# Forgetting attention and a GELU MLP: decay weights by a reversed product scan, v's first pieces among the first loads

## The chip, the cores and the metric

The kernel runs on one core of a Trainium2 chip. The metric is the device time of one execution in microseconds (us). Four executions of the kernel before took 341.31, 341.33, 342.79 and 345.06 us; their median is 342.06. The span is the time between the first and the last instruction in a profiled execution.

The core has five engines that run side by side and meet only at semaphores: TensorE (PE, matrix products; its weight loads are listed apart as PEld), VectorE (DVE), ScalarE (ACT, activation functions), GpSimd (POOL) and SyncE (SP, which here only issues transfers). Each engine takes its own instructions strictly in the order in which the program wrote them. Transfers (DMA) are issued by SP or by POOL and are then carried out by 16 DMA engines that all queues share.

## The reference

Attention over 8 batches, 8 heads, 576 positions and 64 dimensions, in which each key is weakened by the product of all forget factors f after it, followed by a two-layer MLP with an exact GELU over all 4608 tokens.

```python
scores = scale * np.matmul(q, k.transpose(0, 1, 3, 2))
log_f = np.log(np.clip(f, 0.0001, 1.0))
cum = np.cumsum(log_f, axis=-1)
decay = cum[:, :, :, None] - cum[:, :, None, :]
scores = np.where(causal, -1000000000.0, scores + decay)
attn = softmax(scores)                     # max-subtracted, written out in full
x = (attn @ v), heads side by side         # 4608 x 512
h = x @ w_in                               # 512 x 2048
out = gelu(h) @ w_out                      # 2048 x 512
```

For one query the term `cum[query]` is the same for every key and cancels in the softmax. What remains is a weight for each key, proportional to `exp(-cum[key])`. Any common factor of these weights cancels too, because the attention output is divided by the sum of the weights.

## The kernel before

**Tiling.** A head has 576 positions, taken as five key blocks of 128 that start at 0, 128, 256, 384 and 448 (`K0`); the last block is used only in its upper half. Heads are handled in pairs, so that a batch has four pairs, `i` = 0 to 3. `scores(b, i, t)` computes one of four score tiles of a pair on PE (keys on partitions, line 299) and applies Exp on ACT (line 309), giving the tiles `e`. There are two PSUM buffers for score tiles, so PE can be at most two tiles ahead of ACT. `attend` multiplies e by the weighted values `vw` (line 330, called AV below), with the weight itself as a 65th column, which gives the sum. `normalize` (lines 343 and 344, DVE) divides by it and gives x. `to_xT` transposes x on PE (line 363) and copies it out (line 366) on DVE or ACT. `gemm1` (line 385) and `gelu` (line 405) follow, then the second GEMM (lines 421, 479 and 517).

**The weights of the keys.** f is loaded for all 64 batch-heads as one tile of 64 x 576. DVE clamps it (line 185), ACT takes Ln (line 186), DVE scans it to a cumulative sum `cum` (line 188), and ACT computes `wk = Exp(cum[288] - cum)` (line 566). Five PE transposes (line 576) put `wk` on the partitions of the keys, and DVE copies it to `wT` (lines 580, 581). `weigh_v(b, i, eng)` (line 268) multiplies v of a pair of heads by `wT` and gives `vw`. For batch 0 pairs 0 and 1 are weighed on DVE, and pairs 2 and 3 on POOL.

**Order of the loads of batch 0.** q and k are loaded by POOL in pairs of heads, in bf16 (line 107). v is loaded by SP in pieces, one for each key block and half of the heads (`load_v`, line 119). SP has no other work at first, so v is held back by hand: a memset of one column of `v_sb` on POOL (line 151) must run before the first piece may overwrite it, and the pieces after it wait in SP's queue. POOL's queue therefore sets when v starts. In the same way POOL's `gate` (line 546), a copy of one column of v, holds the loads of `w_in` back until v's last piece for heads 0 to 3 has landed.

**Order of the first attention.** `first_attention` is one order written by hand. Warm-up matmuls run on PE until q arrives; then come the transposes of q and k of pair 0 (`transposes_first`, line 207, with copies at 216 to 221), scores of pair 0, transposes of pair 1, and so on. Each engine's order follows the order of the calls. Near the end the calls are `to_xT` of pairs 0 and 1, AV of head (3,0), `to_xT` of pair 2, AV of head (3,1), and the start of GEMM 1, which transposes x of pair 3 in between (`gemm1_begin`). Batches 1 to 7 interleave scores and AV with the second GEMM of the batch before; their code is unchanged.

Of the kernel before, what the change touches and what calls it, by code (L numbers as in the profile page):

```python
# [20 lines left out]
K0 = [0, 128, 256, 384, 448]  # L21
# [31 lines left out]
def kernel(  # L53
# [41 lines left out]
    def load_qk_tokens(b, h0=0, h1=H, which="qk"):  # L95

        if b >= B:
            return
        if b not in qk_of:
            qk_of[b] = [  # L100
                qk_pool.tile([PT, H, JT * D], BF16, tag=n, name=f"{n}{b}")
                for n in "qk"
            ]
        for n, src, dst in zip("qk", (q, k), qk_of[b]):
            if n not in which:
                continue
            nc.gpsimd.dma_start(  # L107
                dst[:, h0:h1, :],
                src[b, h0:h1].rearrange("h (p j) d -> p h (j d)", j=JT),
            )  # L110

    v_sb = consts.tile([P, H, NBLK, D], FP32)

    def load_v(b, h0=0, h1=H):
        if b >= B:
            return
        for n in range(NBLK):
            p0 = D if n == NBLK - 1 else 0
# [29 lines left out]
    diagonal(key_of, Alu.not_equal, 1.0, D)  # L148
    ident_bf = key_of[:, D : D + P]
    load_qk_tokens(0, 4, 6)  # L150
    nc.gpsimd.memset(v_sb[:, :, 0, 0:1], 0.0)
    load_v(0, 0, 4)
    diagonal(after, Alu.is_ge, -1.0e9, D)
    e4 = [consts.tile([P, 2, 448], BF16, name=f"e4{i}") for i in range(4)]
    for t in e4:
        nc.gpsimd.memset(t[:, :, 0:D], 0.0)
    diagonal(ident_fp, Alu.not_equal, 1.0, 0)
    load_qk_tokens(0, 6, 8)
    load_v(0, 4, 8)

    qT = [consts.tile([P, S], BF16, name=f"qT{i}") for i in range(HP)]
    kT = [consts.tile([P, S], BF16, name=f"kT{i}") for i in range(HP)]
# [13 lines left out]


    wT = consts.tile([P, NBLK, BH], FP32)
    ones = consts.tile([BH, S], FP32)
    lf = f_sb  # L180
    cum = consts.tile([BH, S], FP32)
    wk = f_sb
    nc.vector.memset(ones, 1.0)
    nc.vector.memset(wT[0:D, 4, :], 0.0)
    nc.vector.tensor_scalar(f_sb, f_sb, 1e-4, 1.0, Alu.max, Alu.min)
    nc.scalar.activation(lf, f_sb, Act.Ln)
    nc.vector.memset(v_sb[0:D, :, 4, :], 0.0)
    nc.vector.tensor_tensor_scan(cum, ones, lf, 0.0, Alu.mult, Alu.add)
    spark = consts.tile([1, 1], FP32)
    nc.scalar.activation(spark, ones[0:1, 0:1], Act.Exp)  # L190

    def warm_up(n):

        ps = m_psum.tile([P, TC], FP32, tag="m", name="ps_w")
        for _ in range(n):
            nc.tensor.matmul(ps, warm[:, 0:P], warm, start=True, stop=True)

    tails = consts.tile([P, n_dm, TC], BF16)

# [1 line left out]
    def transposes_first(b, i, which, pool, tag):  # L201

        src = qk_of[b][which]
        ps = pool.tile([P, JT, PT], BF16, tag=tag, name="ps_f")
        for j in range(JT):
            for h in range(2):
                nc.tensor.transpose(  # L207
                    ps[h * D : (h + 1) * D, j, :],
                    src[:, 2 * i + h, j * D : (j + 1) * D],
                    ident_bf[:PT, :PT],  # L210
                )

        dst = (qT, kT)[which][i].rearrange("d (p j) -> d p j", j=JT)
        src = ps.rearrange("d j p -> d p j")
        if b or i:
            nc.vector.tensor_copy(dst, src)
        elif which:
            nc.vector.tensor_copy(dst[:, 0 : PT // 2], src[:, 0 : PT // 2])
            nc.scalar.copy(dst[:, PT // 2 :], src[:, PT // 2 :])
        else:  # L220
            nc.scalar.copy(dst, src)
# [41 lines left out]
    def weigh_v(b, i, eng=nc.gpsimd):  # L263

        hs = slice(2 * i, 2 * i + 2)
        bh = b * H + 2 * i
        w = wT[:, :, bh : bh + 2].rearrange("p n h -> p h n")
        eng.tensor_tensor(  # L268
            vw(b)[:, hs, :, 0:D],
            v_sb[:, hs, :, :],  # L270
            w.unsqueeze(3).to_broadcast([P, 2, NBLK, D]),
            Alu.mult,
        )
        if b:
            eng.tensor_copy(vw(b)[:, hs, :, D], w)
# [277 lines left out]
    def first_attention():  # L553


        def transposes(i, pool, tag):
            transposes_first(0, i, 0, pool, tag)
            transposes_first(0, i, 1, pool, tag)

        def attend_head(i, h):  # L560
            attend(0, i, h, (0, 1, 2, 3, 4))
            normalize(0, i, h)

        warm_up(9)
        transposes(0, o_psum, "o")
        nc.scalar.activation(
            wk, cum, Act.Exp, bias=cum[:, S // 2 : S // 2 + 1], scale=-1.0
        )
        warm_up(2)
        scores(0, 0, 0)  # L570
        scores(0, 0, 1)
        transposes(1, m_psum, "m")
        scores(0, 0, 2)
        psw = o_psum.tile([P, NBLK, BH], FP32, tag="o", name="psw")
        for n in range(NBLK):
            nc.tensor.transpose(
                psw[:, n, :], wk[:, K0[n] : K0[n] + P], ident_fp[:BH, :BH]
            )
        scores(0, 0, 3)
        nc.vector.tensor_copy(wT[:, 0:4, :], psw[:, 0:4, :])  # L580
        nc.vector.tensor_copy(wT[D:P, 4, :], psw[D:P, 4, :])
        nc.vector.tensor_copy(
            vw(0)[:, :, :, D], wT[:, :, 0:H].rearrange("p n h -> p h n")
        )
        scores(0, 1, 0)
        transposes(2, m_psum, "m")
        scores(0, 1, 1)
        scores(0, 1, 2)
        scores(0, 1, 3)
        transposes_first(0, 3, 0, m_psum, "m")  # L590
        scores(0, 2, 0)
        transposes_first(0, 3, 1, m_psum, "m")
        weigh_v(0, 0, nc.vector)
        weigh_v(0, 1, nc.vector)
        gate(0, 4)
        load_w_in(0)
        load_w_in(1)
        weigh_v(0, 2)
        weigh_v(0, 3)
        load_w_in(2)  # L600
        nc.gpsimd.memset(v_sb[:, :, 0, 0:1], 0.0)
        load_v(1, 0, 4)
        load_w_in(3)
        load_qk_tokens(1, 0, 4)
        load_qk_tokens(1, 4, 8)
        load_w_out(0)
        scores(0, 2, 1)
        heads = [(i, h) for i in range(3) for h in range(2)]
        for i, t in ((2, 2), (2, 3), (3, 0), (3, 1), (3, 2), (3, 3)):
            scores(0, i, t)  # L610
            attend_head(*heads.pop(0))
        to_xT(0, 0, nc.vector.tensor_copy)
        to_xT(0, 1, nc.scalar.copy)
        attend_head(3, 0)
        both = s_psum.tile([P, 2, 1024], BF16, tag="s", name="ps_x2")
        to_xT(0, 2, nc.scalar.copy, ps=both[:, 0, 0:XC])
        attend_head(3, 1)
        gemm1_begin(0, both)

# [196 lines left out]
```

## Time and profile before

| | us |
|---|---|
| median of four executions | 342.06 |
| the profiled execution | 341.31 |
| its span | 339.5 |
| first attention, to the first full run of GEMM 1 | 0 to 24.9 |
| PE busy in the whole span | 325.1 |
| ACT busy in the whole span | 209.9 |

Stages are read by the time from the start of the span. The profile of the kernel gives the busy time of each engine, the span in 40 slices, and a chain of waits: beginning with the last instruction, it goes back at each step to what released it. The timeline lists instructions in order of time: start, duration, engine, line, operation, tile written and tile read, their shapes, how many were merged into the row, and in brackets the idle time of the engine before it and what ended that time. A duration of a merged row covers all its instructions. The lines on transfer queues give packets, megabytes, and the time that the packets took as a share of 16 engines' time; q0 is POOL's queue and q1 is SP's.

Transfers of the first loads, from issue to landing, by the answers on transfers: q and k of pair 0 were issued at 1.40 and 2.21 and landed after 3.6 and 3.5 us; pair 1 at 2.83 and 3.45, after 4.3 and 4.4; pair 2 at 4.71 and 5.37, after 4.2 and 4.6; pair 3 at 7.22 and 7.87, after 5.2 and 6.5. f was issued at 0.81 and landed after 2.9. The five pieces of v for heads 0 to 3 were issued by SP one after another until 9.8, and took 4.3 to 6.6 us each.

### The profile page before, as it was taken

The page shows a single profiled execution, that of the slowest core. Times are in us where ns is not written, and L with a number is a line of the kernel's source. Part 1 is how long each engine was busy: PE and PEld are TensorE (multiplying, and loading weights), DVE is VectorE, ACT ScalarE, POOL GpSimd, SP SyncE. Part 2 cuts the span into 40 slices and gives each one's busy share as a digit, 9 for nine tenths or more (in the row PEclk, how much of TensorE's full clock was granted, in tenths as well). Part 3 has the DMA queues.
Part 4 walks back from the last instruction along what each step waited for, and adds up shares of the span by engine and source line. Part 5 has one row for each costly group of instructions (what it writes and reads, how often), then busy time and mean ns, then how long its engine had stood idle before and what let it go on. Part 6 is the DMA issues. An engine that isn't in the chain of part 4 may idle for free.

```text
span 339.5 us, 7794 instructions
## 1 busy us (share of the span) xinstructions
PE 325.1 (96%) x3129; PEld 171.6 (51%) x3170; DVE 184.2 (54%) x417; ACT 209.9 (62%) x299; POOL 121.8 (36%) x250
## 2 busy tenths in 40 slices
PE   8699899999999999999999999999999999999995
PEld 4574455445554456445654565446544654444443
DVE  5770456664358935895579646974696541020011
ACT  6977786773734787368737873787368755404600
POOL 8180386037337043723453344524351420000000
PEclk9999999999999999999999999999999999999999
DMA  7999999979999799398959598769900231011013
GB/s 113 184 175 193 209 184 116 217 139 175 216 176 181 112 196 192 96 139 126 229 130 139 106 212 165 97 118 220 159 32 2 82 78 45 0 63 64 0 38 88
DMA packets 104628, 44.18 MB, mean 130 GB/s; under 512 B 83408, under 2 KB 100048, under 8 KB 104592
## 3 DMA queue, kind: packets, MB, share of 16 engines
q1 hardware_dynamic: 87296, 29.52, 46.0%
q0 software_dynamic: 16896, 13.63, 26.8%
q8 instruction: 25, 0.41, 0.5%
q10 hardware_dynamic: 400, 0.52, 0.4%
q14 instruction: 11, 0.09, 0.1%
HBM read 36.85 MB, written 9.44 MB: 136 GB/s over the span
## 4 chain that ended last, share of the span: by engine, by line
PE 89%; issue 3%; ACT 2%; SPq 1%; POOL 1%; DVE 1%; DMA 1%; POOLq 0%; ACTq 0%
PE ps L385 36%; PE ps L479 26%; PE o L330 10%; PE ps L421 8%; PE s L299 7%; ACT e L309 2%; PE ps L517 2%; SPq L119 1%; DMA v_sb<-in_v_dram 1%; PE ps_x L363 1%; POOL q L107 1%; POOL k L107 0%; PE ps_f L207 0%; DVE x L344 0%; DVE vw L268 0%
## 5 line engine op out<-in xcount | busy, mean ns | idle before, releaser
L405 ACT ACTIVATE g<-ps 128x512 bf16<-128x512 f32 x144 | 82.1, 601 | 80.3 <-PE ps L385 80.3
L309 ACT ACTIVATE e<-s 128x896 bf16<-128x896 f32 (+2 forms) x128 | 100.9, 834 | 27.0 <-PE s L299 25.0
L385 PE MATMUL ps<-xT,w_in_sb 128*128 128x512 bf16 x502 | 111.8, 379 | 0.5
L479 PE MATMUL ps<-w_out_sb,g 64*128 64x512 bf16 (+1 forms) x712 | 101.9, 376 | 0.8 <-issue 0.5
L385 PEld LDWEIGHTS <-w_in_sb 128*128 128x128 bf16 x576 | 56.0, 98 | 67.5 <-issue 1.8
L311 POOL TENSOR_SCALAR_AFFINE_SELECT e<-e 128x256 bf16<-128x256 bf16 (+1 forms) x135 | 49.1, 383 | 95.0 <-ACT e L309 94.6
L479 PEld LDWEIGHTS <-g 64*128 64x128 bf16 (+1 forms) x736 | 41.9, 94 | 39.8 <-issue 9.0
L299 PE MATMUL s<-qT,kT 64*128 64x320 bf16 (+4 forms) x384 | 45.4, 276 | 3.3 <-ACT e L309 2.0
L268 POOL TENSOR_TENSOR vw<-v_sb,wT 128x640 bf16<-128x640 f32 x30 | 38.6, 1286 | 23.7 <-DMA v_sb<-in_v_dram 15.2
L249 DVE COPY qT<-tq 64x288 bf16<-64x288 bf16 x96 | 41.4, 431 | 2.9 <-DMA tq<-q 1.5
L249 DVE COPY kT<-tk 64x288 bf16<-64x288 bf16 x96 | 41.5, 432 | 2.5 <-DMA tk<-k 0.9
L487 DVE COPY ot<-ps 128x512 f32<-128x512 f32 x25 | 17.3, 692 | 41.9 <-PE ps L479 41.9
L330 PE MATMUL o<-vw,e 128*128 128x65 bf16 x960 | 36.6, 194 | 3.4 <-issue 2.4
L330 PEld LDWEIGHTS <-e 128*128 128x128 bf16 x960 | 34.1, 98 | 7.3 <-POOL e L311 2.5
L344 DVE TENSOR_TENSOR x<-o,r 128x320 bf16<-128x320 f32 x64 | 31.4, 491 | 2.2
L430 DVE COPY ot<-ps 128x512 f32<-128x512 f32 (+2 forms) x9 | 5.7, 632 | 48.9 <-PE ps L421 46.1
L299 PEld LDWEIGHTS <-kT 64*128 64x128 bf16 x384 | 19.7, 94 | 23.8 <-issue 11.2
L421 PE MATMUL ps<-w_out_sb,g 128*128 128x512 bf16 (+2 forms) x142 | 27.9, 355 | 0.1
L343 DVE RECIPROCAL r<-o 128x5 f32<-128x5 f32 x64 | 12.1, 189 | 22.9 <-PE o L330 22.7
L421 PEld LDWEIGHTS <-g 128*128 128x128 bf16 x144 | 13.5, 98 | 14.5
L490 DVE TENSOR_TENSOR ot<-ot,ps 128x512 f32<-128x512 f32 x25 | 17.2, 687 | 1.4
L385 PE MATMUL ps<-tails,w_in_sb 128*128 128x512 bf16 x62 | 14.2, 377 | 0.2
(67 smaller groups left out, 133.3 us busy)
## 6 DMA issues: line engine op xcount, KB each, us to landing
out_dram<-ot SPq DMA_DIRECT2D x32, 256.0 KB, 2.6
v_sb<-in_v_dram SPq DMA_DIRECT2D x24, 256.0 KB, 4.9
q<-in_q_dram POOLq DMA_DIRECT2D x6, 576.0 KB, 6.4
k<-in_k_dram POOLq DMA_DIRECT2D x6, 576.0 KB, 8.4
v_sb<-in_v_dram SPq DMA_DIRECT2D x22, 128.0 KB, 4.9
w_in_sb<-in_moe_w_in_dram POOLq DMA_DIRECT2D x4, 512.0 KB, 8.4
w_out_sb<-in_moe_w_out_dram POOLq DMA_DIRECT2D x4, 512.0 KB, 8.7
q<-in_q_dram POOLq DMA_DIRECT2D x4, 144.0 KB, 4.2
```

The source lines that it names most:

```text
L249: nc.vector.tensor_copy(rows[:, odd], src[odd * D : (odd + 1) * D, 2 * i + h].rearrange("d j p -> d p j"),)
L268: eng.tensor_tensor(vw(b)[:, hs, :, 0:D], v_sb[:, hs, :, :], w.unsqueeze(3).to_broadcast([P, 2, NBLK, D]), Alu.mult,)
L299: nc.tensor.matmul(to, *ab, start=half < 0, stop=half == 1 or not masked)
L309: nc.scalar.activation(et[:, :, z:c], st[:, :, z:c], Act.Exp, scale=scale)
L311: nc.gpsimd.affine_select(out=et[:, :, c0 + z : c0 + P], in_=et[:, :, c0 + z : c0 + P], compare_op=Alu.is_ge, fill=0.0, base=z, pattern=[[ ...
L330: nc.tensor.matmul(o[:, m, :], e_of[b, i, t][:, h, c : c + P], vw_of[b][:, 2 * i + h, n, :], start=(n == 0), stop=(n == m),)
L344: nc.vector.tensor_tensor(x_of[b, i][:, :, h, :], o[:, :, 0:D], r.unsqueeze(2).to_broadcast([P, NBLK, D]), Alu.mult,)
L385: nc.tensor.matmul(ps, w_in_sb[:, kt, ffb * P : (ffb + 1) * P], src[:, kt, 0:TC], start=(kt == 0), stop=(kt == n_dm - 1),)
L405: nc.scalar.activation(g_of[c][ffb], ps, Act.Gelu)
L421: nc.tensor.matmul(pss[ts][:, c0:c1], g_of[c][kt][:, ts * P : (ts + 1) * P], w_out_sb[:, kt, c0:c1], start=(kt == 0), stop=(kt == n_ff - 1),)
L479: nc.tensor.matmul(banks[r], g_of[c][kt][rows, ts * P : (ts + 1) * P], w_out_sb[rows, kt, :], start=kt == (steps.index("r") if r else 0), ...
L487: nc.vector.tensor_copy(ot, banks[1])
```

## The change

The decay weights become a product. Since common factors cancel, the weight of a key may be the product of all later f, which one scan gives when it runs backwards: `decay[575] = 2**80`, `decay[s-1] = decay[s] * f[s]`. The scan reads f and writes `decay` through reversed views; its added operand is a tile of zeros, `none`. Ln, `cum` and the Exp at line 566 go, and the spark, a one-element Exp that loads ACT's table, comes first. The factor 2**80 keeps products of up to 575 factors in the range of the type.

The memsets of `e4`, and those that hold v back, move from POOL to DVE. `load_v` gets a parameter that selects key blocks. Blocks 0 and 1 of heads 0 to 3 are issued after a DVE memset near the start; blocks 2 to 4 and the second half of the heads after another, which stands behind the scan. On POOL, q and k of pair 3 are issued right after the mask `after`, ahead of `ident_fp`. In the first attention the second warm-up has 256 columns, `weigh_v(0, 0)` stands ahead of the transposes and the copy of k of pair 3, and `to_xT` of pair 2 stands ahead of AV of head (3,0).

```diff
-    def load_v(b, h0=0, h1=H):
+    def load_v(b, h0=0, h1=H, ns=range(NBLK)):
...
-        for n in range(NBLK):
+        for n in ns:
...
     load_qk_tokens(0, 4, 6)
-    nc.gpsimd.memset(v_sb[:, :, 0, 0:1], 0.0)
-    load_v(0, 0, 4)
     diagonal(after, Alu.is_ge, -1.0e9, D)
-    e4 = [consts.tile([P, 2, 448], BF16, name=f"e4{i}") for i in range(4)]
-    for t in e4:
-        nc.gpsimd.memset(t[:, :, 0:D], 0.0)
+    load_qk_tokens(0, 6, 8)
     diagonal(ident_fp, Alu.not_equal, 1.0, 0)
-    load_qk_tokens(0, 6, 8)
-    load_v(0, 4, 8)
...
-    ones = consts.tile([BH, S], FP32)
-    lf = f_sb
-    cum = consts.tile([BH, S], FP32)
-    wk = f_sb
-    nc.vector.memset(ones, 1.0)
+    none = consts.tile([BH, S], FP32)
+    decay = consts.tile([BH, S], FP32)
+    nc.vector.memset(none, 0.0)
+    spark = consts.tile([1, 1], FP32)
+    nc.scalar.activation(spark, none[0:1, 0:1], Act.Exp)
+    nc.vector.memset(v_sb[:, 0:4, 0, 0:1], 0.0)
+    load_v(0, 0, 4, (0, 1))
+    nc.vector.memset(v_sb[0:D, :, 4, :], 0.0)
     nc.vector.memset(wT[0:D, 4, :], 0.0)
+    nc.vector.memset(decay[:, S - 1 : S], 2.0**80)
+    e4 = [consts.tile([P, 2, 448], BF16, name=f"e4{i}") for i in range(4)]
+    for t in e4:
+        nc.vector.memset(t[:, :, 0:D], 0.0)
     nc.vector.tensor_scalar(f_sb, f_sb, 1e-4, 1.0, Alu.max, Alu.min)
-    nc.scalar.activation(lf, f_sb, Act.Ln)
-    nc.vector.memset(v_sb[0:D, :, 4, :], 0.0)
-    nc.vector.tensor_tensor_scan(cum, ones, lf, 0.0, Alu.mult, Alu.add)
-    spark = consts.tile([1, 1], FP32)
-    nc.scalar.activation(spark, ones[0:1, 0:1], Act.Exp)
-
-    def warm_up(n):
+    nc.vector.tensor_tensor_scan(
+        decay[:, S - 2 :: -1],
+        f_sb[:, S - 1 : 0 : -1],
+        none[:, 0 : S - 1],
+        2.0**80,
+        Alu.mult,
+        Alu.add,
+    )
+    nc.vector.memset(v_sb[:, 0:4, 2, 0:1], 0.0)
+    load_v(0, 0, 4, (2, 3, 4))
+    load_v(0, 4, 8)
+
+    def warm_up(n, w=TC):
...
         transposes(0, o_psum, "o")
-        nc.scalar.activation(
-            wk, cum, Act.Exp, bias=cum[:, S // 2 : S // 2 + 1], scale=-1.0
-        )
-        warm_up(2)
+        warm_up(2, 2 * P)
...
-                psw[:, n, :], wk[:, K0[n] : K0[n] + P], ident_fp[:BH, :BH]
+                psw[:, n, :], decay[:, K0[n] : K0[n] + P], ident_fp[:BH, :BH]
...
         scores(0, 2, 0)
+        weigh_v(0, 0, nc.vector)
         transposes_first(0, 3, 1, m_psum, "m")
-        weigh_v(0, 0, nc.vector)
         weigh_v(0, 1, nc.vector)
...
         to_xT(0, 1, nc.scalar.copy)
-        attend_head(3, 0)
         both = s_psum.tile([P, 2, 1024], BF16, tag="s", name="ps_x2")
         to_xT(0, 2, nc.scalar.copy, ps=both[:, 0, 0:XC])
+        attend_head(3, 0)
         attend_head(3, 1)
```

More of the change, by code (lines that the diff above doesn't have):

```diff
@@ L178 @@
     wT = consts.tile([P, NBLK, BH], FP32)
-    ones = consts.tile([BH, S], FP32)
-    lf = f_sb
-    cum = consts.tile([BH, S], FP32)
-    wk = f_sb
-    nc.vector.memset(ones, 1.0)
+    none = consts.tile([BH, S], FP32)
[6 more added lines that the diff above has]
+    nc.vector.memset(v_sb[0:D, :, 4, :], 0.0)
     nc.vector.memset(wT[0:D, 4, :], 0.0)
+    nc.vector.memset(decay[:, S - 1 : S], 2.0**80)
+    e4 = [consts.tile([P, 2, 448], BF16, name=f"e4{i}") for i in range(4)]
+    for t in e4:
+        nc.vector.memset(t[:, :, 0:D], 0.0)
     nc.vector.tensor_scalar(f_sb, f_sb, 1e-4, 1.0, Alu.max, Alu.min)
-    nc.scalar.activation(lf, f_sb, Act.Ln)
-    nc.vector.memset(v_sb[0:D, :, 4, :], 0.0)
-    nc.vector.tensor_tensor_scan(cum, ones, lf, 0.0, Alu.mult, Alu.add)
-    spark = consts.tile([1, 1], FP32)
-    nc.scalar.activation(spark, ones[0:1, 0:1], Act.Exp)
-    def warm_up(n):
+    nc.vector.tensor_tensor_scan(
[10 more added lines that the diff above has]
+    def warm_up(n, w=TC):
         ps = m_psum.tile([P, TC], FP32, tag="m", name="ps_w")
         for _ in range(n):
-            nc.tensor.matmul(ps, warm[:, 0:P], warm, start=True, stop=True)
+            nc.tensor.matmul(
+                ps[:, 0:w], warm[:, 0:P], warm[:, 0:w], start=True, stop=True
+            )
     tails = consts.tile([P, n_dm, TC], BF16)
```

## The prediction

> **What bounds the kernel now.** I begin with the page's busy table, its slices and its chain.
>
> ```profile
> span 339.5 us, 7794 instructions
> ...
> PE 325.1 (96%) x3129; PEld 171.6 (51%) x3170; DVE 184.2 (54%) x417; ACT 209.9 (62%) x299; POOL 121.8 (36%) x250
> ...
> PE   8699899999999999999999999999999999999995
> ...
> PE 89%; issue 3%; ACT 2%; SPq 1%; POOL 1%; DVE 1%; DMA 1%; POOLq 0%; ACTq 0%
> ```
>
> TensorE (PE) is busy for 96% and carries 89% of the chain. No edit takes real work from PE except 0.3 us of warm-up, so the change can win only where PE waits. Every edit acts before 24.4 us. I therefore read busy time by stage (first attention to 24.4 us, GEMM 1 of batch 0 to 37): PE is busy 4.74 of the first 6.00 us, 7.34 of the next 9.24, 8.00 of the 9.16 up to 24.40, then 12.52 of 12.60. All that could be had is about 4 us, 1.2% of the run. From 24.4 us on PE runs full, and a shift there travels to the end.
>
> Next the chain of waits cut to the first 42 us:
>
> ```profile
> 11.71 3.88 DMA v_sb<-in_v_dram
> 15.60 0.01 issue
> 15.61 0.83 DVE vw L268
> 16.44 0.04 issue
> 16.49 0.63 PE o L330 x15
> ...
> 23.88 0.50 DVE x L344
> 24.38 0.05 issue
> 24.42 0.45 PE ps_x L363 x5
> 24.88 9.81 PE ps L385 x45
> ```
>
> So until 16.49 the end is set by transfers and by the first weighing of v. The timeline shows what holds that weighing:
>
> ```profile
> 14.45 0.45 PE L207 MATMUL ps_f<-key_of,k 96*64 96x96 bf16 x12 [0.54 <-DMA k<-in_k_dram]
> 14.94 0.76 DVE L216 COPY kT<-ps_f 128x576 bf16<-128x576 bf16 x1 [0.80 <-PE ps_f L207]
> 15.02 0.19 POOL L546 COPY gate<-v_sb 64x1 f32<-64x1 f32 x1 [6.52 <-DMA v_sb<-in_v_dram]
> 15.24 1.62 ACT L309 ACTIVATE e<-s 128x768 bf16<-128x768 f32 x2 [0.37 <-PE s L299]
> 15.40 0.10 PEld L330 LDWEIGHTS <-e 128*128 128x128 bf16 x1
> 15.61 1.55 DVE L268 TENSOR_TENSOR vw<-v_sb,wT 128x640 bf16<-128x640 f32 x2
> 16.49 0.63 PE L330 MATMUL o<-vw,e 128*128 128x65 bf16 x15 [1.02 <-DVE vw L268]
> ```
>
> The reader is to see three things. The gate at 15.02 shows that v for heads 0 to 3 has landed, so the chain's word "DMA" at 15.60 is a guess. The weighing begins when DVE is through with the copy of kT before it (14.94 + 0.76). And PE had everything else by 15.40, since it had loaded its weights: it lost 16.49 - 15.40 = 1.09 us to DVE's order.
>
> **The change, part by part.** Durations and the sum go against the profiled execution, 341.31 us (span 339.5 and 1.8 around it).
>
> Decay without Ln. ACT loses the Ln table load (1.28 us at 0.81, in idle time), Ln itself (0.68), the second load (1.28 at 4.88, for Exp; one load remains, now ahead) and the Exp of 0.77 us at 7.09. The first copy of qT at 6.28 stood behind that second load and the spark (6.17 + 0.20), though q's transposes ended at 5.90; the first e at 7.76 stood behind the Exp, though its scores were through by 7.58. If k came as before, the first e would start at 7.3 to 7.6, worth 0.15 to 0.45 us. The scan over 575 reversed elements replaces one over 576 (1.35 us). f lands at 3.69, the clamp takes 0.45, so the scan ends near 5.6 instead of 6.24; the weights are read by PE at 8.9, 3 us later. A reversed operand is in no row; between the same 1.35 and double, 2.70, it stays hidden but for the kT copy of DVE at 6.27, which the doubled scan would delay by 0.7 us. I take 1.35, the row of the same instruction.
>
> Memsets moved to DVE. Ahead of the clamp DVE has idle time from 2.30 to 3.69. Added there: four e4 (217 ns on POOL; 165 for as many bytes twice over on DVE), v's tail (485, from behind the clamp), two tiny ones (about 100): 1.2 to 1.5 us for 1.39 free. Free to +0.1 us of scan, nothing at the end. "none" replaces "ones". POOL loses four times 0.16 and 0.13, so q and k of pair 3 are issued at about 6.4 and 7.1, not 7.22 and 7.87.
>
> Warm-up of 256 columns for 512: -0.3 us of PE at 6.16, hidden behind the copies of qT and kT.
>
> v's first two pieces early. SP (0.51 us each) issues them at about 2.4, after a DVE memset, instead of 6.47; f needed some 1.7 us from issue to first packet in the transfers' slices, so they move from about 4.3. They are 1024 of the 2304 packets of 256 B (4 heads x 576 rows) in half of v. All first loads keep the 16 engines full from 3 us (112% of share from 4 to 8 us), so v takes time from q and k of pairs 0 to 2, and what it takes comes back later: pair 3 and v's rest are nearer done. How two queues share is shown twice, first from 10 to 13 us, then from 24 to 38:
>
> ```profile
> q0 software_dynamic: 399, 0.28, 63.1%
> q1 hardware_dynamic: 1563, 0.39, 62.2%
> ...
> q0 software_dynamic: 2508, 2.09, 92.8%
> q1 hardware_dynamic: 2345, 0.58, 31.8%
> ```
>
> With q0 deep in work (the second pair) v gets one packet for one, 167 per us, and q0 keeps 93/112 of its pace, so q and k are stretched by 20%. In the first pair v gets four for one, and q and k go at half pace. Packets from 4.3 us on: in the first way k of pair 0 lands near 5.9 (5.71 before), k of pair 1 near 8.4 (7.85), k of pair 2 near 10.8 (9.97), k of pair 3, issued earlier, near 12.5 (14.37); v of heads 0 to 3 near 13.2 (14.9). In the second way k of pairs 0 and 1 comes 0.6 and 1.1 us late and pair 3 near 13. ACT's row of nine exponentials ran without a gap from 7.76 to 14.86, and the second would have to wait for k of pair 1 only beyond 8.7. So the cost in front is 0 to 0.6 us of ACT's row, against the 0.15 to 0.45 won above. I take nothing for both together; the early queue is deep as in the second sharing row, so the first way is nearer.
>
> The Trainium skill, page "DMA: Bandwidth & Descriptors", section "Queues, rings and completion order", speaks against this edit: each DMA engine goes round the queues that have work, packet by packet, so early v would take turns from the very q and k that gate the start. By that rule, read as equal turns per record, the sum is the first way; the first of the two rows does not agree with it.
>
> v's rest: the second memset sits on DVE behind the scan, so SP goes on near 5.7 rather than 6.6. It waits for f on the way; nothing else is queued on SP.
>
> weigh_v(0,0) ahead of the last kT copy. DVE copies qT of pair 3 (0.76, from 13.38 at the latest), then weighs (0.82) if v is there (13.2 to 14.9), so it is done between 14.97 and 15.75; the kT copy comes after and is needed only by scores of pair 3, past 16.5. PE starts attending at 15.40 (everything else is ready) instead of 16.49: -1.09 us; -0.7 if v lands at 14.9. ACT allows it: from 15.24 it has 1.62 + 0.70 + 3.45 = 5.77 us of exponentials, so it could end at 21.0 rather than at 21.99.
>
> POOL's gate opens with v, near 13.3, and w_in goes out up to 1.7 us earlier, so that all later loads move with PE.
>
> x of pair 2 ahead of the last AV. AV of head (2,1) ended at 21.82, its normalization (0.20 + 0.49 and gaps) at 22.58; PE finished the transposes of pairs 0 and 1 at 22.38. The moved transposes must wait for 22.62, where before AV (3,0) filled that time: +0.24 us, and PE holds AV (3,0) and (3,1) behind them. What they free, ACT's copy of xT, is not late now: ACT's Gelu waits 0.83 us for PE at 25.99. Bounds: 0 if AV (3,0) would be waiting for its exponentials anyway, +0.5 if ACT's copy of pair 1 comes in between.
>
> Sum: 0 - 1.09 + 0.24 = **-0.85 us**, so 341.31 - 0.85 = **340.5 us**, with -1.5 (all of ACT's lead kept) and +0.1 (v no sooner, k late) as this case's bounds: 339.8 to 341.4. Two of the four runs of before lie within 0.02 us of the profiled one and the median, 342.06, is 0.75 above it, so I give the fast time and leave the rest to the range.
>
> **Rivals.**
> A. Nothing gained: the loads bind, not the order. For it: the engines are full to 15 us and the bytes are the same. Then k of pair 3 and v land as before, the late k of pairs 1 and 2 costs ACT 0.4, the x move costs 0.24, and reordering returns 0.7: about 341.3. Against it: pair 3 is issued 0.8 us sooner, and v's second half can be last.
> B. More than forecast: k of pair 0 is not delayed, the e row starts at 7.4 and nothing else stalls: -1.5, 339.8. Against it: the early v.
> C. Slower: w_in in front of v's second half. If v's first half lands by 11, POOL opens the gate then, and w_in flows from about 2.4 us later (15.48 to 17.9 before). v of heads 4 to 7 would then run one for one at 167 packets per us for the 5 us of two w_in chunks, in place of some 900 per us alone (243 GB/s from 12 to 14 us, over 256 B). It decides from the point where that half lands after 17.9: AV (2,0) at 19.2 needs POOL's weighing of 1.28. Full price +2.8 on AV (2,0), less the gain: 343.3 to 343.8.
> D. PE slow for longer: its first matmuls of 512 columns come 0.42 us apart, later ones 0.22. A longer wait for k of pair 0 and less warm-up could put that step off by some us while ACT already paces PE: +1 to 2, 342.5 to 343.3.
>
> **How the numbers follow.** Forecast 0.52, A 0.25, B 0.08, C 0.10, D 0.05. The range takes in B's better half and most of C and D: 339.4 to 342.9. One per cent, 3.4 us, is about what a measurement of this kernel can tell from no change; only C with D, or something unseen in the loads, passes it upward (0.05), and the 4 us that PE waits at all cannot come near it downward (0.02). Within: 0.93.
>
> **What would show it.** Right: first AV on PE near 15.4 with no wait for vw; no ACT gap at 15; k of pair 3 landing near 12.5; v's first pieces taking longer than 4.3 us; a wait of about 0.25 us ahead of the third group of x transposes; GEMM 1 of batch 0 from 23.9 rather than 24.7, and the same lead at the end. Wrong: ACT gaps between 8 and 12 (late k), POOL waiting for v beyond 17.9 (C), or first AV still past 16 us.

## The result

The changed kernel is a little slower. Its executions have a median of 342.42 us (53 of them); those of the kernel before 341.47 us (79). The ratio is 1.0025, with a 95% interval of 1.0013 to 1.0037. That lies within 1%, as forecast, and within the range. The sign is wrong: 0.85 us less was forecast, and about 0.85 us more was measured (0.25% of 341.47).

The chain of waits of the changed kernel, cut to its first 42 us (start, duration, what), has these pieces where the kernel before had the landing of v and the first weighing:

```profile
7.66 7.57 DMA k<-in_k_dram
...
15.28 0.45 PE ps_f L216 x12
...
23.71 0.49 DVE x L353
...
24.34 0.50 DVE x L353
...
24.89 0.45 PE ps_x L372 x5
25.34 9.81 PE ps L394 x45
```

The wait has moved from v to k of pair 3, which lands at 15.26 (14.37 before, forecast 12.5). GEMM 1 of batch 0 then begins its full run at 25.34; it was 24.88, and the forecast was 0.85 us earlier. The loss is made in the last 4 us of this stretch. AV of head (2,1) still begins 0.12 us ahead of before (21.05 against 21.17). Behind it two normalizations (23.71 and 24.34) now stand one behind the other in the chain, where before only one did.

The timeline of the changed kernel in front:

```profile
3.88 1.35 DVE L187 TENSOR_TENSOR_SCAN decay<-f_sb,none 64x575 f32<-64x575 f32 x1
4.16 1.27 POOL L138 TENSOR_SCALAR_AFFINE_SELECT key_of<-key_of 128x256 bf16<-128x256 bf16 x1
5.47 0.45 PE L216 MATMUL ps_f<-key_of,q 96*64 96x96 bf16 x12 [0.40 <-POOL key_of L138]
14.47 0.82 DVE L277 TENSOR_TENSOR vw<-v_sb,wT 128x640 bf16<-128x640 f32 x1
15.28 0.45 PE L216 MATMUL ps_f<-key_of,k 96*64 96x96 bf16 x12 [0.94 <-DMA k<-in_k_dram]
16.06 5.80 ACT L318 ACTIVATE e<-s 128x768 bf16<-128x768 f32 x7 [0.78 <-PE s L308]
16.23 0.65 PE L339 MATMUL o<-vw,e 128*128 128x65 bf16 x15
```

In the kernel before, the scan and the select (a masked fill on POOL that makes `key_of`) were these:

```profile
4.37 0.41 POOL L138 TENSOR_SCALAR_AFFINE_SELECT key_of<-key_of 128x256 bf16<-128x256 bf16 x1
...
4.89 1.35 DVE L188 TENSOR_TENSOR_SCAN cum<-ones,f_sb 64x576 f32<-64x576 f32 x1 [0.21 <-ACT f_sb L186]
```

The scan costs what it did (1.35 us) and is early, and v is weighed at 14.47, before the last k has landed. The select of key_of on POOL takes 1.27 us instead of 0.41, and holds what stands behind it on POOL: q and k of pair 2 are issued 0.67 us later than before. ACT waits 0.78 us for scores that wait for k.

Landings in us, from the answers on transfers of the profiled executions (two of the experiments are told further down):

| | before | after | early v alone | scan behind key_of | forecast |
|---|---|---|---|---|---|
| k of pair 0 | 5.71 | 6.29 | 6.31 | 6.48 | 5.9 |
| k of pair 1 | 7.85 | 8.74 | 8.16 | 9.13 | 8.4 |
| k of pair 2 | 9.97 | 11.23 | 9.78 | 10.43 | 10.8 |
| k of pair 3 | 14.37 | 15.26 | 13.08 | 13.48 | 12.5 |
| v, heads 0 to 3 | 14.86 | 11.63 | 11.72 | 13.98 | 13.2 |

The landing of the last k differs between executions by about as much as the table's columns differ. With the loads of the kernel before (five profiles) it lies between 13.5 and 14.4, and with those of the changed kernel (six profiles) between 14.2 and 15.3: 14.37 and 15.26 are each at the late end. With early v alone (two profiles) it lies at 13.1 and 13.8, and with the scan behind key_of (three) between 13.1 and 13.8.

One profile is one execution, and this one flatters the changed kernel: its span is 339.6 us (before 339.5). The mean granted clock of an execution also varies, from 1.0 down to 0.979, so "at full clock" below means executions over 0.9965, and their median is given beside the ratio: before 341.43 us (118 of 158 executions, 95% interval 341.29 to 341.57), after 342.15 (341.91 to 342.39). Their median spans are 339.3 and 340.1 us. So 0.7 us of the difference is there in executions whose mean granted clock is full.

### The profile page after: what moved, and what is told of

Read it like the earlier page. It is cut to its first block, busy times and chain, and to the rows that moved or that the text cites. A ratio compares the mean times of both kernels' runs of the same rounds, so it can differ in the third digit from the quotient of the medians.

```text
span 339.6 us, 7791 instructions
## 1 busy us (share of the span) xinstructions
PE 324.9 (96%) x3129; PEld 171.4 (50%) x3170; DVE 184.3 (54%) x424; ACT 207.7 (61%) x296; POOL 122.0 (36%) x245
## 4 chain that ended last, share of the span: by engine, by line
PE 90%; issue 2%; DMA 2%; ACT 2%; POOL 2%; DVE 1%; POOLq 0%; ACTq 0%
PE ps L394 36%; PE ps L488 26%; PE o L339 10%; PE ps L430 8%; PE s L308 7%; DMA k<-in_k_dram 2%; ACT e L318 2%; PE ps L526 2%; POOL q L107 1%; PE ps_x L372 1%; DVE x L353 1%; PE ps_f L216 1%; POOL k L107 0%; DVE qT L225 0%; DVE r L352 0%
## 5 line engine op out<-in xcount | busy, mean ns | idle before, releaser
L258 DVE COPY kT<-tk 64x288 bf16<-64x288 bf16 x96 | 42.6, 444 | 1.7
L258 DVE COPY qT<-tq 64x288 bf16<-64x288 bf16 x96 | 40.1, 418 | 1.4
L430 PEld LDWEIGHTS <-g 128*128 128x128 bf16 x144 | 13.5, 98 | 14.5
L394 PE MATMUL ps<-tails,w_in_sb 128*128 128x512 bf16 x62 | 14.2, 377 | 0.2
```

The lines of the kernel that those rows point to most:

```text
L258: nc.vector.tensor_copy(rows[:, odd], src[odd * D : (odd + 1) * D, 2 * i + h].rearrange("d j p -> d p j"),)
L394: nc.tensor.matmul(ps, w_in_sb[:, kt, ffb * P : (ffb + 1) * P], src[:, kt, 0:TC], start=(kt == 0), stop=(kt == n_dm - 1),)
L430: nc.tensor.matmul(pss[ts][:, c0:c1], g_of[c][kt][:, ts * P : (ts + 1) * P], w_out_sb[:, kt, c0:c1], start=(kt == 0), stop=(kt == n_ff - 1),)
```

## The experiments

In what was expected, T is the theory at that point and R its rival. Landmarks are compared by the first matmul of each head's AV.

### Undoing one part of the change

The moved x back behind AV (3,0):

```diff
-        to_xT(0, 2, nc.scalar.copy, ps=both[:, 0, 0:XC])
         attend_head(3, 0)
+        to_xT(0, 2, nc.scalar.copy, ps=both[:, 0, 0:XC])
         attend_head(3, 1)
```

> The changed kernel with one edit undone: x of pair 2 is transposed behind AV of head (3,0) again. Theory T (three debits: the moved x, POOL's select of key_of held up by DVE's earlier scan, early v in front of q and k): the move runs AV (3,0) and (3,1) back to back behind a wait and leaves both normalizations to DVE at the end, so it costs 0.5 to 0.6 us; x of pair 3 is transposed at 24.3 to 24.4 instead of 24.89, and the time is 0.5 us under that of the changed kernel, within 0.3 us of before. Rival R (early v alone; the move costs only its wait): 0.25 us under the changed kernel, x of pair 3 at 24.65.

Measured: x of pair 3 is transposed at 24.39, ratio to before 1.0012 (0.9987 to 1.0038), 341.03 us at full clock (eight executions, 340.88 to 341.59): 1.1 us under the changed kernel. T's landmark is met; the time falls by more than the 0.5 us that the landmark explains, and by how much more is uncertain by the interval.

All of v behind the scan:

```diff
-    nc.vector.memset(v_sb[:, 0:4, 0, 0:1], 0.0)
-    load_v(0, 0, 4, (0, 1))
...
-    nc.vector.memset(v_sb[:, 0:4, 2, 0:1], 0.0)
-    load_v(0, 0, 4, (2, 3, 4))
+    nc.vector.memset(v_sb[:, 0:4, 0, 0:1], 0.0)
+    load_v(0, 0, 4)
```

> The changed kernel without early v: all five pieces of heads 0 to 3 stand behind the scan. T: k of pair 0 lands near 5.8 instead of 6.3, but q's transposes still wait for key_of until 5.45 and q and k of pair 2 are still issued at 5.4 and 6.0; first e near 7.75, k of pair 3 near 14.2; 0.3 to 0.4 us under the changed kernel. R: all that was lost in front comes back, k of pair 3 near 13 and no gap of ACT at 15; 0.8 us or more under the changed kernel.

Measured: ratio 1.0030 (1.0002 to 1.0059), 342.18 us at full clock, no better than the changed kernel. The first e starts at 7.9 and AV at 16.38, but transposes of k of pair 2 only at 11.99, and the nine exponentials now take 8.0 us with gaps. k of pair 3 is transposed at 15.05. Both expectations miss: with the select still long, taking v out of the way pays nothing that these six executions at full clock show.

Clamp and scan behind the select of key_of:

```diff
+    held = consts.tile([1, 1], BF16)
...
+    nc.vector.tensor_copy(held, key_of[0:1, 0:1])
     nc.vector.tensor_scalar(f_sb, f_sb, 1e-4, 1.0, Alu.max, Alu.min)
```

> The changed kernel with a one-element DVE copy of key_of ahead of the clamp, so that clamp and scan begin only when POOL's select of key_of is through. T: the select takes 0.41 us instead of 1.27, q and k of pair 2 are issued 0.65 us earlier, at 4.7 and 5.35, q's transposes start at 5.1, the scan ends near 6.4; the first e starts 0.1 to 0.3 us earlier, k of pair 3 lands 0.3 to 0.6 earlier; 0.3 to 0.5 us under the changed kernel. R: the select still takes 1.2 us or its length does not matter; within 0.15 us of the changed kernel.

Measured: the select takes 0.41 us, q and k of pair 2 are issued at 4.49 and 5.23 (5.38 and 6.03 in the changed kernel), k of pair 3 lands at 13.48 instead of 15.26. First AV at 16.07 (16.23), and x of pair 3 is transposed at 24.62 (24.89), so the edit gains 0.27 us at 25 us. 341.44 us at full clock (seven executions, 341.04 to 342.75), 0.7 under the changed kernel but not clear of it; over all executions 1.0013 (0.9981 to 1.0044). The edit does a second thing: v's later pieces wait for the scan, which now ends at 6.48 instead of 5.23, so q and k also have less of v beside them. The first e comes no sooner (8.31): early v holds k of pair 0 to 6.48.

### What holds the select

The scan's added zeros, read from PSUM instead of SBUF:

```diff
-    none = consts.tile([BH, S], FP32)
+    none = m_psum.tile([BH, TC], FP32, tag="m", name="none")
...
-        none[:, 0 : S - 1],
+        none[:, 0:1].to_broadcast([BH, S - 1]),
```

> The changed kernel with the scan's added zeros read from PSUM (one column, broadcast) instead of from SBUF; the old tile's memset stays, so that DVE's times in front don't move. T-port (the select is held up because the scan reads two SBUF operands beside it): the select of key_of takes 0.41 us although clamp and scan still run at 3.4 to 5.3; q and k of pair 2 are issued near 4.6 and 5.25, q's transposes begin near 5.1. R-port (something else of the earlier clamp and scan, or of the queue, holds it): it still takes 1.2 to 1.35 us.

Measured, in the timeline of this kernel:

```profile
4.08 1.34 DVE L189 TENSOR_TENSOR_SCAN decay<-f_sb,none 64x575 f32<-64x575 f32 x1
4.27 0.41 POOL L138 TENSOR_SCALAR_AFFINE_SELECT key_of<-key_of 128x256 bf16<-128x256 bf16 x1
```

Scan and select run side by side as in the changed kernel, and the select takes 0.41 us. So it is the scan's second operand in SBUF that holds POOL, and not the earlier time of the scan. (The edit also makes that operand one column read over and over; the two were not tried apart.) In the changed kernel's two profiles the select ends 0.20 and 0.19 us after the scan (5.43 against 5.23, 5.54 against 5.35), as if it stood until the scan was through. The Trainium skill states this rule, "SBUF — State Buffer", section "Who interferes with whom": a VectorE instruction with two SBUF inputs contends with a GpSimd instruction that reads SBUF, and the order of issue decides which of the two is held. This case agrees, at 0.41 against 1.27 us. It also corrects the description of the core ahead of the prediction: the engines do not meet only at semaphores.

In this profile only the select is short, and v's later pieces go out early as in the changed kernel. There k of pair 3 is issued at 6.90 (7.66 in the changed kernel) and lands at 14.30, against 13.1 to 13.8 with the scan behind key_of. So the select alone does not account for the 13.48 above. The same execution ran at half the granted clock from 8.6 to 22.3 us, so its time (345.68) says nothing on the edit.

### One part alone in the kernel before

The moved x alone (the first edit, the other way round, in the kernel before):

> The kernel before with one edit: x of pair 2 transposed ahead of AV of head (3,0). T: 0.5 us lost between 21.5 and 25 us: the transposes wait 0.25 us for x of head (2,1), AV (3,0) and (3,1) then run back to back and their two normalizations stand one behind the other on DVE; x of pair 3 at 24.9 instead of 24.42, 0.5 us over before. R: 0.25 us, the wait alone: x of pair 3 at 24.67.

Measured: the profiled execution was late before this stretch (half the granted clock from 18.6 to 22.0 us), so the stretch itself is compared. From AV (2,1) to the transposes of x of pair 3 it takes 3.85 us, as in the changed kernel (3.84); before, and with x back, 3.25. So the move costs 0.60 us there. 341.82 us at full clock (341.51 to 342.05), 0.4 over before; over all executions 1.0004 (0.9972 to 1.0036). The timeline of the changed kernel shows the mechanism:

```profile
22.52 0.45 PE L372 MATMUL ps_x<-key_of,x 128*128 128x128 bf16 x5 [0.26 <-DVE x L353]
22.81 1.11 PE L339 MATMUL o<-vw,e 128*128 128x65 bf16 x30
23.48 0.20 DVE L352 RECIPROCAL r<-o 128x5 f32<-128x5 f32 x1 [0.62 <-PE o L339]
24.34 0.49 DVE L353 TENSOR_TENSOR x<-o,r 128x320 bf16<-128x320 f32 x1
24.89 0.45 PE L372 MATMUL ps_x<-key_of,x 128*128 128x128 bf16 x5 [0.32 <-DVE x L353]
```

PE waits 0.26 us, as forecast, but then runs 30 matmuls of two heads without a break. DVE, idle for 0.62 us, gets both heads at the end, and x of head (3,1) is ready 0.92 us after its AV. In the kernel before the transposes stood between the two heads, and the first normalization was over when the second head was done:

```profile
22.97 0.64 PE L330 MATMUL o<-vw,e 128*128 128x65 bf16 x15
...
23.12 0.49 DVE L344 TENSOR_TENSOR x<-o,r 128x320 bf16<-128x320 f32 x1
...
23.88 0.49 DVE L344 TENSOR_TENSOR x<-o,r 128x320 bf16<-128x320 f32 x1
```

The weighing alone:

```diff
+        weigh_v(0, 0, nc.vector)
         transposes_first(0, 3, 1, m_psum, "m")
-        weigh_v(0, 0, nc.vector)
```

> The kernel before with one edit: the first weighing of v ahead of the last k's transposes and copy. T: DVE weighs at 14.95, when v has landed, instead of 15.61; first AV at 15.85 instead of 16.49; 0.5 to 0.7 us under before. R2: ACT's row of exponentials and k of pair 3 at 14.4 pace what follows, and the earlier AV is given back by 22 us: within 0.2 us of before.

> The kernel before with the weighing of v ahead of the last k, once more. T: first AV near 15.5, about 1.0 us ahead of before at 25 us, and the lead stays to the end where no later transfer of x is late; 0.5 to 1.0 us under before. R2: the lead of 1.0 us is given back at one place behind 200 us as in the first profile, with PE waiting for the transposed x, so that it is a wait of this order and not a chance one.

Measured: first AV at 15.45 and 15.70 (16.49 before), GEMM 1 of batch 0 ahead by 1.02 and 0.7 us; 340.88 and 341.26 us at full clock, ratios 0.9985 (0.9951 to 1.0019) and 0.9991 (0.9964 to 1.0017). The lead is there and most of it is gone at the end, in the two profiles at two different places. In the first, 1.17 us go near 244 us, where PE waits for a transposed x:

```profile
244.60 1.70 PE L385 MATMUL ps<-xT,w_in_sb 128*128 128x512 bf16 x6 [0.60 <-DMA xT<-x]
```

In the second, 1.1 us go between 49 and 54 us of batch 1, where POOL waits for v, its masks stand behind that weighing, and PE's AV behind the masks:

```profile
48.91 1.28 POOL L268 TENSOR_TENSOR vw<-v_sb,wT 128x640 bf16<-128x640 f32 x1 [1.85 <-DMA v_sb<-in_v_dram]
...
53.09 1.33 PE L330 MATMUL o<-vw,e 128*128 128x65 bf16 x28 [0.69 <-POOL e L311]
```

So R2's one place is refuted, and T's lead to the end as well: in both profiles the lead ends at a transfer that was not earlier.

Early v alone (with the parameter of `load_v`, and the memset of `ones` moved ahead):

```diff
+    nc.vector.memset(v_sb[:, 0:4, 0, 0:1], 0.0)
+    load_v(0, 0, 4, (0, 1))
     diagonal(key_of, Alu.not_equal, 1.0, D)
...
-    nc.gpsimd.memset(v_sb[:, :, 0, 0:1], 0.0)
-    load_v(0, 0, 4)
+    nc.gpsimd.memset(v_sb[:, :, 2, 0:1], 0.0)
+    load_v(0, 0, 4, (2, 3, 4))
```

> The kernel before with one edit: v's first two pieces (heads 0 to 3) issued at about 2.4 behind a DVE memset, the rest where it was. T (two queues share two packets of v for one of q and k in front, as the changed kernel's profile has it): k of pair 0 lands at 6.3 instead of 5.7 and k of pair 1 at 8.7 instead of 7.85; the first e starts 0.3 to 0.5 us later, the first AV at 16.5 to 16.9; 0.2 to 0.5 us over before. R (the loads' order costs nothing by itself, v's earlier landing pays for it): within 0.1 us of before at 25 us, or ahead of it.

Measured: k of pair 0 lands at 6.31, the first e starts at 8.30 (7.76 before), k of pair 3 lands 1.3 us earlier (13.08), first AV at 16.42. At 25 us it is level with before, within 0.06, as R has it; yet 342.13 us at full clock (341.83 to 342.47), 0.7 over before, as T has it. Ratio 1.0021 (0.9996 to 1.0045). Where the executions lose it, this profile does not show.

### When the two weighings meet

The changed kernel once more:

> The changed kernel once more, for a second profile: its first one has a span of 339.6, while its executions at full granted clock have a median span of 340.1, and 21 of its 54 executions show a granted clock under 0.9965. T-clock (the clock step of the front moves from execution to execution, and the change leaves PE idler there): 3 to 7 of 12 under 0.9965, and the landmarks of the front (k of pair 0, the late k of pair 3, the x move's 0.5 us) within 0.3 us of the first profile. R (the first profile was an odd one): landmarks of the front 0.5 us or more later in this one at the same clock.

Measured: ratio 1.0029 (1.0004 to 1.0053), median 342.91. Three of 12 executions are under 0.9965. The profile differs from the first by more than expected. Its timeline:

```profile
6.43 0.69 PE L216 MATMUL ps_f<-key_of,k 96*64 96x96 bf16 x12
...
16.47 3.10 POOL L277 TENSOR_TENSOR vw<-v_sb,wT 128x640 bf16<-128x640 f32 x2 [2.38 <-DVE vw L277]
16.74 1.70 DVE L277 TENSOR_TENSOR vw<-v_sb,wT 128x640 bf16<-128x640 f32 x1
...
19.12 0.65 PE L339 MATMUL o<-vw,e 128*128 128x65 bf16 x15 [0.51 <-DVE x L353]
```

Two things are late here that the first profile does not have. The transposes of k take 0.69 us where the first profile had 0.45: PE still runs at half pace, and its full granted clock is recorded from 10.0 us on (4.7 in the first profile, 5.8 in the one of before). And DVE's second weighing takes 1.70 us, because POOL began its own 0.27 us ahead of it; both have two operands in SBUF. Early v lets POOL begin sooner (16.28 with early v alone, 17.07 before). In the first profile DVE came first, and the longer time was POOL's (2.84 us for two, 2.52 before):

```profile
16.44 0.82 DVE L277 TENSOR_TENSOR vw<-v_sb,wT 128x640 bf16<-128x640 f32 x1
16.79 2.84 POOL L277 TENSOR_TENSOR vw<-v_sb,wT 128x640 bf16<-128x640 f32 x2 [3.02 <-DVE kT L225]
```

In the second profile GEMM 1 of batch 0 begins 1.28 us later than before.

POOL's weighing held behind DVE's second:

```diff
         load_w_in(1)
+        done = x_pool.tile([P, 1], FP32, tag="gate", name="gate")
+        nc.gpsimd.tensor_copy(done, vw(0)[:, 2, 0, 0:1])
         weigh_v(0, 2)
```

> The changed kernel with a one-column POOL copy of vw of pair 1 ahead of POOL's weighing of pair 2, so that POOL begins only when DVE's second weighing is through. T-meet (the two weighings read SBUF through one port and the later one stands still, which in most executions is DVE): DVE's second weighing takes 0.82 us, POOL's first 1.28, AV (1,0) starts 1.05 us after AV (0,1) at most; the executions at full clock have a median span of 339.5 to 339.7 instead of 340.1, the median time is 0.4 to 0.7 us lower than the changed kernel's. R: as the changed kernel, 340.1.

Measured: 0.82 and 1.28 us, AV (1,0) 1.05 us behind (0,1), span at full clock 339.6, 341.78 us (after 342.15); over all 1.0013 (0.9978 to 1.0047). As expected of T-meet in the spans, but only seven executions are at full clock (341.33 to 344.85). Here k of pair 3 lands at 14.21, and the first AV begins at 15.78.

The same edit in the kernel with early v alone:

> The kernel before with v's first two pieces early, and POOL's weighing held behind DVE's second one. T-meet: both weighings at 0.82 and 1.28 us, never beside each other; the first AV and GEMM 1 of batch 0 level with before at 25 us, within 0.2 us; the median at full clock comes back from 342.1 (early v alone) to 341.3 to 341.6, where before is. R (late k of pairs 0 and 1 costs it): stays at 342.0 or more.

Measured: 342.46 us at full clock, ratio 1.0005 (0.9983 to 1.0027). Early v's cost does not come from the meeting: R. In its profile k of pair 0 is transposed at 6.54 after a wait of 0.56 us, still at half pace (0.69), full clock is recorded from 9.8 us on, and the first e starts at 9.04.

### How busy PE is in front

Six matmuls of 512 columns in PE's waits (`keep_warm(n)` runs n of them into a PSUM tile that nobody reads):

```diff
-        transposes(0, o_psum, "o")
+        transposes_first(0, 0, 0, o_psum, "o")
+        warm_up(1)
+        transposes_first(0, 0, 1, o_psum, "o")
...
+        keep_warm(1)
         scores(0, 1, 0)
...
+        keep_warm(1)
         scores(0, 1, 2)
...
         scores(0, 2, 0)
+        keep_warm(3)
```

in the changed kernel, in the weighing alone, and in the kernel called best (below):

> The changed kernel with six more warm-up matmuls of 512 columns in PE's waits before the first AV: one between q's and k's first transposes, one each ahead of two score tiles of pair 1, three ahead of the last k's transposes. T-clock: dips go (0 to 2 of 12 executions under 0.9965, where the changed kernel has 39%), the median falls by 0.3 to 0.6 us, and the landmarks stay within 0.3 us of the changed kernel's. R: dips have nothing to do with how busy PE is in front; 4 to 6 of 12, and the time is the same or 0.2 us more.

> The kernel before with the first weighing ahead of the last k, and the same six extra matmuls. T-clock: 0 to 2 of 12 under 0.9965; GEMM 1 of batch 0 0.8 to 1.0 us ahead of before at 25 us; 0.8 to 1.2 us under before in the median, and clear of it. R: 3 to 4 of 12 as the weighing alone had, and no better than it, 0.2 to 0.5 us under before.

> The kernel called best (no early v, x back, DVE's scan behind key_of) with the same six extra matmuls. T-clock: 0 to 2 of 12 under 0.9965 and a median 0.5 to 1.0 us under before. The first AV is again near 16.5, because v lands behind pair 3. R: as best without them, 0.2 to 0.5 us under before, with dips as often.

Measured: 2, 0 and 1 of 12 executions under 0.9965, together 3 of 36; the same three kernels without the extra work had 24 of 66, 5 of 24 and 2 of 12. That is what T-clock expected, but it does not yet show that dips depend on how busy PE is in front: run beside them, the changed kernel without the extra work had 3 of 12, and elsewhere early v with POOL's weighing behind had none of 12. And no time is won: 342.62, 341.73 and 341.66 us at full clock, ratios 1.0028 (1.0009 to 1.0047), 0.9986 (0.9964 to 1.0007) and 0.9995 (0.9974 to 1.0016). In the weighing kernel the extra matmuls delay the transposes of k of pair 0 from 5.71 to 6.38 and the last k's from 13.99 to 15.21. Whether the changed kernel dips more often than before is not settled: 24 of 66 against 40 of 158.

### Debits taken out together

Scan behind key_of and x back; the same with v behind the scan; the first with POOL's weighing behind DVE's; and x back with POOL's weighing behind, the scan where it was:

> The changed kernel with two debits taken out: DVE's clamp and scan wait for key_of, and x of pair 2 is back behind AV (3,0); early v stays. T: first e still at 8.2 to 8.3, since early v holds k of pair 0 to 6.4; first AV near 16.07; GEMM 1 of batch 0 runs 0.35 us ahead of before at 25 us; 0.3 to 0.5 us under before. R (early v alone costs what is lost): no better than before.

> As the kernel with two debits taken out, and early v taken out as well (all five pieces behind the scan, which ends near 6.4): what stays of the change are the product scan without Ln, pair 3 issued earlier, the shorter warm-up and the weighing ahead of the last k. T: k of pair 0 at 5.75, first e at 7.5 to 7.7, k of pair 3 at 13.7 to 14, first AV at 15.2, GEMM 1 of batch 0 some 1.2 us ahead of before at 25 us; 1.0 to 1.2 us under before where no later transfer is late. R: the weighing alone had 1.02 us at 25 us, and no Ln adds nothing, since k of pair 3 and ACT's row pace the rest: 1.0.

> The changed kernel with three debits taken out: clamp and scan behind key_of, x of pair 2 back behind AV (3,0), POOL's weighing behind DVE's; early v stays. T: first e at 8.2, first AV near 16.1, GEMM 1 of batch 0 0.3 to 0.5 us ahead of before at 25 us; 0.3 to 0.6 us under before at full clock (before: 341.5 median of those). R: no better than before.

> The changed kernel without the moved x and with POOL's weighing behind DVE's; early v, the product scan beside key_of's select and the weighing order stay. T: first AV at 15.8 to 16.2, GEMM 1 of batch 0 0.3 to 0.8 us ahead of before at 25 us; median at full clock 340.6 to 341.0, 0.4 to 0.8 us under before. R: x_back's 341.0 already had what is to be had; no better than that, 341.0 to 341.3.

| | ratio (95% interval) | at full clock, us | first AV in the profile |
|---|---|---|---|
| key_x_back | 1.0021 (0.9985 to 1.0057) | 341.58 | 18.72, half clock from 7.4 to 21 us |
| best | 0.9983 (0.9956 to 1.0010) | 341.51 | 16.60 |
| three_out | 1.0025 (0.9995 to 1.0054) | 341.55 | 16.78, half clock from 7.9 to 11.4 |
| two_out | 1.0026 (0.9996 to 1.0056) | 341.66 | 16.70, half clock from 8.6 to 12.0 |

Measured: all four are within 0.25 us of before at full clock (5, 10, 7 and 5 executions), and R is nearer than T in each. The gains of the single edits at full clock (1.1 with x back, 0.7 with the scan behind key_of, 0.4 with POOL's weighing behind) do not add up: the three together gain 0.6, less than x back alone. These medians of few executions do not divide the loss among the parts; the landmarks of the profiles are the firmer evidence. In best k of pair 3 lands at 13.48 but v of heads 0 to 3 only at 15.64: pair 3, issued earlier, stands ahead of it. No kernel of this study beats before clear of its interval.

## Why the prediction was wrong

**Which terms failed.** The sum was 0 for the loads and the scan, -1.09 for the weighing and +0.24 for the moved x. At 25 us the first profile of the changed kernel is at +0.46 instead of -0.85. In its terms: the weighing brought -0.26 at the first AV, since k of pair 3 had not landed, and the moved x cost 0.60. The remaining 0.1 us arises between the two. The steps that failed are therefore the loads at nothing ("I take nothing for both together", with the last k near 12.5) and the size of the moved x. That a loss at 25 us becomes the 0.7 us of the executions at full clock is not shown: the two profiles of the changed kernel end 0.1 and 0.9 us behind before in their spans.

**The product scan and the memsets.** The durations were right: 1.35 us for the reversed scan, DVE free 0.24 us before f landed. What failed is "the scan ends near 5.6 ... 3 us later ... hidden". The cover was looked for in who reads the weights, not in what runs beside the scan. Moved from 4.89 to 3.88, the scan met POOL's select of key_of: +0.86 us on POOL, q and k of pair 2 issued 0.67 us later, and q's first transposes held for 0.40 us. With the scan behind key_of, 0.27 us come back at 25 us. The forecast had no such term. How much of the last k's late landing belongs to it, and how much to v's pieces beside it, is not separated.

**Early v.** The step "the early queue is deep as in the second sharing row, so the first way is nearer" failed. The transfers of the changed kernel from 4 to 8 us:

```profile
q0 software_dynamic: 712, 0.50, 85.3%
q1 hardware_dynamic: 1431, 0.36, 41.2%
```

That is two packets of v for one of q or k, between the two rows that were shown. k of pair 0 came 0.6 us late, as in the way that was not taken. That what is taken comes back later is seen in early v alone (13.1 and 13.8 for the last k, 13.5 to 14.4 before), but not in the changed kernel (14.2 to 15.3). Early v is the one part whose cost alone is clear of the intervals at full clock (0.7 us, and 1.0 with POOL's weighing behind); by the ratios over all executions it is not (1.0021 and 1.0005, both intervals taking in 1).

**No Ln.** The 0.15 to 0.45 us in front were not seen: the first e starts at 8.13 (7.76), since k of pair 0, not ACT's tables, is last. The kernel called best has no early v, and there too the first e starts only at 7.73, after 0.44 us of waiting for PE's scores.

**The weighing.** The mechanism was right, -1.09 us: alone it brought the first AV forward by 1.04 and 0.79 us, and GEMM 1 by 1.02 and 0.7. It needs the last k: PE's order has the transposes of that k ahead of the first AV. Where k landed at 15.26 the first AV began at 16.23, and where it landed at 14.21 (POOL's weighing behind) at 15.78. In the second profile k landed at 14.39, but the exponentials ran late behind PE's half pace (first e at 8.65), and the first AV began at 16.59. The step "from 24.4 us on PE runs full, and a shift there travels to the end" holds only roughly: of the +0.46 and +1.28 us at 25 us, 0.1 and 0.9 are left in the spans, and the weighing's gain met late transfers in both profiles, so that 0.55 and 0.17 us of it remained in the medians at full clock.

**The moved x.** The term of +0.24 us was mis-sized: 0.60 us. The wait was right (0.26); that both normalizations then pile up on DVE ahead of x of pair 3 was not in the sum.

**The rivals.** A's condition came true in half: the last k did not land sooner than before, though v did. Its price, 341.3, had the moved x at 0.24. B needed k of pair 0 on time, and it was 0.6 us late. C's condition nearly held: v's first half landed at 11.63 and the gate opened at 11.77, but the second half was there in time; POOL began its weighing at 16.79. What came of it in some executions was the meeting of the two weighings. D, given 0.05, has the price nearest to the 342.42, and is seen in some executions: full clock only from 10 us on, or half clock again after 7 to 9 us, in six of the twelve profiles with early v. In the eight without it full clock is recorded from 4.9 to 7.0 us on, with one later dip each in two of them (at 18.6 and at 43 us). That early v's longer wait for k causes this is argued from these profiles, not shown: early v alone had only 2 dips in 12. How the 0.7 us of early v alone divide between late k and the late clock step stays open.

**Slips in the working.** The range up to 342.9 leaves out all of C (343.3 to 343.8) and half of D, though the text says that it takes in most of both. D's +1 to 2 us on 341.31 are 342.3 to 343.3. The scores of the first e were through at 7.63 by their row, not by 7.58. None of these bears on the miss.

## What to carry to other kernels

An instruction moved earlier has to be checked against what the other engines run at its new time, not only against its own inputs: VectorE with two SBUF operands and GpSimd reading SBUF held each other up here, at the select and again at the two weighings. Where a short piece of work is moved to fill a wait, look at what it separated: the transposes between two heads gave DVE its time. And a gain of 1 us at the start is worth only what the next loads leave of it. Before a landing time is compared between two kernels, look at how far it moves between executions of one: here by about 1 us.

## What the runs showed of the hardware

In the clock records of the 20 profiles PE's full pace begins at 3.9 to 10.0 us, from execution to execution of much the same front. A stretch in which PE was busy for 2.14 of 3.40 us (the kernel with zeros in PSUM, 5.2 to 8.6 us) was followed by 13.65 us at half the granted clock, in an execution with a span of 343.8 us. The mean granted clock of an execution does not show a late first step: the second profile of the changed kernel has 1.0 with full clock from 10.0 us on. "TensorE: Matmul & The Clock Gate" of the Trainium skill, section "Part 1: The HAM clock gate", states the free-running window of about 3.4 us that this looks like; the recorded stretches of 3.41 us (three_out, 7.94 to 11.35) and 13.65 us, four times as long, agree with it.
